# Moving the gating-weight loads of a fused attention and gated-MLP kernel to ScalarE's DMA queue, with a new timetable for the attention units

## The chip, the cores and the metric

The kernel runs on one core of one Trainium2 chip, in one launch. The metric is the device time of that launch in microseconds (us). Everything is computed in fp32; where a product needs it, an operand is split into a rounded part ("hi") and the rest ("lo"), and three matmuls (hi·hi, hi·lo, lo·hi) stand for one.

## The reference

Chunked attention in 8 heads over 4608 tokens (8 sequences of 576, chunks of 64, head size 64), then an RMS norm and a gated MLP (model width 512, inner width 1536):

```python
scores = scale * np.matmul(q_c, k_c.transpose(0, 1, 2, 4, 3))     # 64x64 per chunk
attn = softmax(scores)
out = np.matmul(attn, v_c)                                        # x: 4608 x 512
xn = x / sqrt(mean(x * x) + 1e-06) * rms_g
g = xn @ w_gate                                                   # 512 -> 1536
result = (silu(g) * (xn @ w_val)) @ w_out                         # 1536 -> 512
```

## The kernel before, in words

**Stages.** The 4608 tokens are nine tiles of 512. The first three ("plain" tiles) go through the MLP as ordinary matrix products. The other six go two by two, as three *pairs*, through a Strassen-Winograd scheme: seven block products P1 to P7 instead of eight. A pair has an *up* part (gate and value weights, `up_pair`, six groups `i` of seven products, 42 *steps*) and a *down* part (output weights, `down_pair`, again 42 steps). In the up part the products of a group come in the order `FIRST` for i = 0 and `ORD` (P1 P6 P5 P7 P2 P4 P3) otherwise, so step s is product s mod 7 of group s // 7. An up step is 12 matmuls of 128x128 by 128x512 (`product`, L751), a down step 6 of them (L925).

**Attention in between.** While a pair is computed, the attention of the next pair's tokens is done in four *units* of 256 tokens, unit 0 to 3. `unit_steps` gives the ten pieces of a unit: load q and k; scores on TensorE, then the two exponentials on ScalarE (`first`, L340); load v; sums and a VectorE transpose (`second`); write the weights to DRAM (`away`, L362, two transfers); read them back turned (`third`, L371, eight transfers); attention values on TensorE (L388) and the norm, which uses VectorE (L402), ScalarE (L455, L410) and GpSimd (`fourth`); a VectorE transpose (L416); write x to DRAM (L421); read it back (L428, four transfers). Unit n starts at up step `PAIR_AT[n]`, and piece k comes at the end of up step `PAIR_AT[n] + PAIR_STEPS[k]`; what falls on step 42 or later goes to down step 2·(step - 42), ahead of that step's product. The last pair has no units.

**Order of work.** In the pairs the order on SyncE's queue (SP), VectorE and ScalarE is the order in which the program is written; TensorE's too. All transfers of the pairs are issued from SP, one after the other: an issue that waits holds back all issues behind it. In the compiled program the transfers, whatever queue issues them, take eight completion counters in turn, and an issue waits until the transfer eight places earlier in the program has landed.

**Weights.** The block weights of the up part lie in DRAM as 21 *rings* (`wsd`, 1 MB, two products each) and are loaded into a pool of 18 buffers (`wts`, 8 KB a partition) that also holds the inputs of the products (`xp`), the gated results (`g`) and the output weights (`wo`). A buffer is taken in the order in which buffers were given back. At the start of each product, `ring_load_ahead(n // 2)` brings the loads up to three rings ahead; from group 1 on this puts one ring load at the start of each even step s, and the ring is first used at step s + 4. The first three rings of the next pair are loaded at down step 34. The output weights are loaded by `out_load` in 14 *slots* per pair of four or two blocks. P5, P6, P7 and P3 come from `wol` in one transfer a slot; P1, P2 and P4 (`AS_IS`) are cut out of `wod` with one transfer of 256 KB per block. `out_load` runs three slots ahead; slots 0 and 1 are loaded at up steps 39 and 41.

**Down part.** Each down step uses a gated block split into hi (ScalarE, `gh`, L848) and lo (VectorE, `gl`, L849). `split_next` runs four ahead: the first four splits are at up steps 35, 37, 39 and 41 (`G_AT`). `less` (L885) adds a VectorE subtraction to down steps 2 to 7, 9 to 14 and 20 to 25. `start(5)` (L1200) is one more VectorE subtraction just before down step 0.

## Time and profile before

| | |
|---|---|
| runs (median, lowest, highest) | 924.67, 922.69, 924.72 us |
| the profiled execution's own time | 925.69 us |
| its span, first to last instruction | 923.9 us |
| granted TensorE clock, mean | 0.996 |
| TensorE matmul busy | 887.3 us (96%) |
| VectorE / ScalarE / GpSimd busy | 644.0 / 444.6 / 127.4 us |
| transfers | 233.41 MB, mean 253 GB/s |
| ring loads `wr<-wsd` | 63 of 1024 KB, median 8.2 us from issue to landing |
| output weights `wo<-wod` | 54 of 256 KB, median 6.9 us |

In the profile's rows, L751 is line 751 of the kernel; `ps_a<-xp,wr` is a matmul into the tile ps_a from xp and wr. PE is TensorE's matmuls, PEld its weight loads, DVE VectorE, ACT ScalarE, POOL GpSimd, SPq the queue of SyncE, ACTq that of ScalarE. A number in brackets with an arrow, `[1.39 <-DMA wr<-wsd]`, is idle time of the engine just before the row, and what ended it. The table of windows has, for each stretch of time, the busy time of each engine with its instructions in brackets, then the granted clock, the busy share of the DMA engines and their rate.

### The profile page before, as it was taken

To read this page: it belongs to the slowest core of one execution; us is meant where nothing else is said; L and a number is where in the kernel's file an instruction comes from. 1 tells how busy PE (TensorE), PEld (TensorE's weight loads), DVE (VectorE), ACT (ScalarE), POOL (GpSimd) and SP (SyncE) were. 2 spreads that over 40 slices of the span, in tenths; PEclk is the share of its full clock that TensorE was granted. 3 is DMA by queue.
4 is the path that set the end of the run, shared out by engine and by line. 5 is a ranking of instruction groups with operands and counts; after the bars stand their busy time and mean duration, and the time that the engine had idled before them with its cause. 6 is when DMAs were issued, how large, how long until landed. Compare 5 with 4: busy or idle time off the path is not lost.

```text
span 923.9 us, 17389 instructions
## 1 busy us (share of the span) xinstructions
PE 887.3 (96%) x6828; PEld 724.4 (78%) x6828; DVE 644.0 (70%) x1071; ACT 444.6 (48%) x731; POOL 127.4 (14%) x141
## 2 busy tenths in 40 slices
PE   5799999999999999999998999999999999999998
PEld 4578878887887878878876788887787888888886
DVE  6999986465587554856775987676589974444885
ACT  5988944353456564433453643344355532212452
POOL 0100012233300000121221000221220002211000
PEclk9999999999999999999999999999999999999999
DMA  9698989877997762668795868478688777345713
GB/s 352 275 330 304 365 314 344 290 248 220 292 328 230 224 187 78 250 228 293 246 326 201 298 260 315 177 251 310 258 283 276 257 286 315 142 141 165 264 47 136
DMA packets 98226, 233.41 MB, mean 253 GB/s; under 512 B 9440, under 2 KB 61152, under 8 KB 85472
## 3 DMA queue, kind: packets, MB, share of 16 engines
q1 hardware_dynamic: 97088, 231.77, 71.4%
q8 instruction: 54, 0.88, 0.4%
q10 hardware_dynamic: 1056, 0.52, 0.2%
q14 instruction: 28, 0.23, 0.1%
HBM read 167.25 MB, written 65.01 MB: 251 GB/s over the span
## 4 chain that ended last, share of the span: by engine, by line
PE 65%; DMA 8%; DVE 5%; ACT 3%; SPq 2%; issue 2%; POOL 2%; ACTq 0%; DVEq 0%; POOLq 0%
PE ps_c L751 9%; PE ps_a L751 9%; PE ps_b L751 9%; PE ps_b L925 5%; PE ps_g L545 5%; PE acc L580 5%; PE ps_v L545 5%; PE ps_d L751 5%; PE ps_c L925 4%; PE ps_a L925 4%; PE ps_d L925 3%; DMA kt<-kT_dram 2%; DMA wo<-wol 2%; PE ps_o L388 1%; DMA away_e<-e 1%
## 5 line engine op out<-in xcount | busy, mean ns | idle before, releaser
L848 ACT CAST gh<-g 128x512 fp32r<-128x512 f32 x126 | 73.6, 619 | 71.4 <-PE ps_b L925 18.9
L751 PE MATMUL ps_a<-xp,wr 128*128 128x512 f32 x432 | 104.1, 390 | 2.3 <-DMA wr<-wsd 2.0
L751 PE MATMUL ps_c<-xp,wr 128*128 128x512 f32 x432 | 106.2, 395 | 0.0
L751 PE MATMUL ps_b<-xp,wr 128*128 128x512 f32 x432 | 103.8, 390 | 0.0
L849 DVE TENSOR_TENSOR gl<-g,gh 128x512 fp32r<-128x512 f32 x126 | 86.0, 687 | 23.2 <-ACT gh L848 21.8
L545 PE MATMUL ps_g<-xh,parts 128*128 128x512 f32 x288 | 98.2, 400 | 3.1 <-ACT sg L563 2.9
L545 PE MATMUL ps_v<-xh,parts 128*128 128x512 f32 x288 | 95.9, 393 | 0.5 <-DVE sg L567 0.5
L751 PEld LDWEIGHTS ps_a<-xp,wr 128*128 128x128 f32 x432 | 80.7, 188 | 19.8 <-issue 3.0
L751 PEld LDWEIGHTS ps_c<-xp,wr 128*128 128x128 f32 x432 | 81.7, 190 | 17.4
L751 PEld LDWEIGHTS ps_b<-xp,wr 128*128 128x128 f32 x432 | 80.8, 188 | 16.9
L580 PE MATMUL acc<-parts,gh 128*128 128x512 f32 x288 | 90.2, 394 | 0.0
L545 PEld LDWEIGHTS ps_g<-xh,parts 128*128 128x128 f32 x288 | 55.1, 191 | 16.3 <-ACT sg L563 4.0
L815 POOL TENSOR_TENSOR g<-c,c 128x512 f32<-128x512 f32 x18 | 23.2, 1290 | 308.8 <-DVE c L811 293.1
L545 PEld LDWEIGHTS ps_v<-xh,parts 128*128 128x128 f32 x288 | 54.7, 190 | 12.5 <-DVE sg L567 1.0
L580 PEld LDWEIGHTS acc<-parts,gh 128*128 128x128 f32 x288 | 53.1, 188 | 11.4 <-ACT gh L568 0.2
L791 ACT ACTIVATE c<-c 128x512 f32<-128x512 f32 x18 | 11.4, 633 | 96.9 <-DVE c L811 96.9
L545 PE MATMUL ps_g<-xl,parts 128*128 128x512 f32 x144 | 57.2, 397 | 0.0
L545 PE MATMUL ps_v<-xl,parts 128*128 128x512 f32 x144 | 56.5, 392 | 0.0
L580 PE MATMUL acc<-parts,gl 128*128 128x512 f32 x144 | 56.3, 391 | 0.0
L751 PE MATMUL ps_d<-xp,wr 128*128 128x512 f32 x216 | 52.2, 390 | 0.0
L567 DVE TENSOR_TENSOR sg<-ps_v,sg 128x512 f32<-128x512 f32 x36 | 24.6, 683 | 32.4 <-PE ps_v L545 28.6
L751 PEld LDWEIGHTS ps_d<-xp,wr 128*128 128x128 f32 x216 | 40.3, 188 | 8.6
(143 smaller groups left out, 1677.4 us busy)
## 6 DMA issues: line engine op xcount, KB each, us to landing
wr<-wsd SPq DMA_DIRECT2D x63, 1024.0 KB, 8.2
wo<-wod SPq DMA_DIRECT2D x54, 256.0 KB, 6.9
raw<-w_up_dram SPq DMA_DIRECT2D x12, 1024.0 KB, 7.8
wo<-wol SPq DMA_DIRECT2D x12, 1024.0 KB, 7.5
vt<-v_dram SPq DMA_DIRECT2D x18, 512.0 KB, 5.8
wsd<-parts SPq DMA_DIRECT2D x18, 512.0 KB, 7.5
qt<-qT_dram SPq DMA_DIRECT2D x17, 512.0 KB, 6.0
kt<-kT_dram SPq DMA_DIRECT2D x17, 512.0 KB, 6.9
```

The source lines that it names most:

```text
L388: nc.tensor.matmul(st["o"][(2 * c + t) * Q : (2 * c + t + 1) * Q, h * D : (h + 1) * D], eT[c][rows, t, h], vt[rows, c, h], start=True, sto ...
L545: nc.tensor.matmul(ps, a[f][:, cols], b[dt], start=(dt == 0 and i == 0), stop=(dt == NDT - 1 and i == 2),)
L567: nc.vector.tensor_tensor(sg, pv, sg, op=ALU.mult)
L580: nc.tensor.matmul(acc[s], a[:, cols], b, start=(f == 0 and i == 0), stop=(f == NF - 1 and i == 2),)
L751: nc.tensor.matmul(ps, w[:, a, m, cols], xp[:, b, kt], start=start and kt == 0 and i == 0, stop=stop and kt == 1 and i == 2, skip_group_ch ...
L791: nc.scalar.activation(t, t if src is None else src, AF.Silu)
L815: nc.gpsimd.tensor_tensor(g[:, 1, 1], kp["c22"], kept[0]["c22"], op=mult)
L848: nc.scalar.copy(gh, src)
L849: nc.vector.tensor_tensor(gl, src, gh.bitcast(F32), op=ALU.subtract)
L925: nc.tensor.matmul(ps[m][INTO[p]], w[:, m, a], parts[c], start=p in FROM and i == 0 and j == 0, stop=p in LAST and i == NPR - 1 and j == 2 ...
```

## The change

The ring loads inside the up part are issued from ScalarE's queue, at the same place in the program (the start of the product). The next pair's first three rings are loaded one by one at down steps 24, 28 and 32, still from SP, instead of all at step 34. `wod` becomes one DRAM tensor, so that a slot of P1, P2 or P4 is one transfer of 1 MB or 512 KB instead of four or two of 256 KB. The units start at steps 3, 13, 23, 33 instead of 5, 14, 23, 32, and the last four pieces of a unit come one step later. With that, unit 3's `fourth` and the VectorE transpose after it move from up steps 40 and 41 to down steps 0 and 2, and its write and read of x from down steps 0 and 2 to 4 and 6. The scaling of the first half of x (`x1`) moves from up steps 35 and 36 to 30 and 31.

```diff
-PAIR_STEPS = -4, 0, 1, 2, 3, 4, 8, 9, 10, 11
-PAIR_AT = 5, 14, 23, 32
+PAIR_STEPS = -4, 0, 1, 2, 3, 4, 9, 10, 11, 12
+PAIR_AT = 3, 13, 23, 33
...
-EARLY_AT = (35, "x1"), (36, "x1")
+EARLY_AT = (30, "x1"), (31, "x1")
...
+RING_AT = 24, 28, 32
...
-    wod = [dram.tile([P, 4 * DM], F32, name=f"wod{n}") for n in range(NPR)]
+    wod = dram.tile([P, NPR, 4 * DM], F32, name="wod")
...
-        nc.sync.dma_start(wod[i], flat(out_parts[i]).bitcast(F32))
+        nc.sync.dma_start(wod[:, i], flat(out_parts[i]).bitcast(F32))
...
-    def ring_load(n):
+    def ring_load(n, queue):
         if n < len(wsd):
             t = ring[n] = big([P, 2, 2, 2, KH], F32R, "wr")
-            nc.sync.dma_start(t.rearrange("p n a m c -> p n (a m c)").bitcast(F32), wsd[n])
+            queue.dma_start(t.rearrange("p n a m c -> p n (a m c)").bitcast(F32), wsd[n])
...
-            ring_load_ahead(n // 2)
+            ring_load_ahead(n // 2, nc.scalar)
...
-    def ring_load_ahead(n):
+    def ring_load_ahead(n, queue=nc.sync):
         while loaded[0] < min(n + AHEAD_R, len(wsd)):
-            ring_load(loaded[0])
+            ring_load(loaded[0], queue)
             loaded[0] += 1
...
         if ns[0][0] in AS_IS:
-            for j, (p, i) in enumerate(ns):
-                part = wod[i].rearrange("p (a n c) -> p a n c", a=2, c=KH)[:, :, AS_IS[p]]
-                nc.sync.dma_start(t[:, j].rearrange("p (a c) -> p a c", a=2).bitcast(F32), part)
+            p, i = ns[0]
+            part = wod[:, i : i + len(ns)].rearrange("p j (a n c) -> p j a n c", a=2, c=KH)
+            to = t[:, : len(ns)].rearrange("p j (a c) -> p j a c", a=2)
+            nc.sync.dma_start(to.bitcast(F32), part[:, :, :, AS_IS[p]])
...
-            down_at.setdefault(7 * NPR - 8, []).append(lambda: ring_load_ahead(0))
+            for n, k in enumerate(RING_AT):
+                down_at.setdefault(k, []).append(lambda n=n: ring_load_ahead(n + 1 - AHEAD_R))
```

## The prediction

> **What bounds the kernel now.** I read the page first (TensorE busy 96% of the span, clock 0.996), then a table of windows with one row for the up part and one for the down part of each pair, because nothing before the first pair changes but six stores.

> ```profile
> core 0: us, PE busy (x) PEld busy (x) DVE busy (x) ACT busy (x) POOL busy (x), PEclk, DMA share, GB/s
> 369.57:503.59 134.02, 128.37 (x1274) 104.46 (x1272) 90.38 (x157) 54.79 (x89) 27.07 (x32) 0.99 0.74 264
> 503.59:561.54 57.95, 57.41 (x253) 47.23 (x252) 50.00 (x75) 31.39 (x52) 0.00 (x0) 1.00 0.73 263
> 561.54:690.14 128.60, 126.94 (x1273) 103.94 (x1272) 89.97 (x157) 52.41 (x84) 26.49 (x32) 1.00 0.75 266
> 690.14:748.62 58.48, 57.57 (x253) 47.15 (x252) 50.00 (x75) 32.57 (x54) 0.55 (x1) 1.00 0.72 252
> 748.62:863.02 114.40, 114.40 (x506) 94.78 (x505) 57.53 (x82) 26.35 (x43) 20.63 (x16) 1.00 0.62 223
> ```

> TensorE is the bound in every row, at full clock. Its idle time is the only thing that a change of order can win: 5.65 us in the first up part, 0.54, 1.66 and 0.91 in the next three, none in the last pair, which has no units. Together 8.8 us. The waits of TensorE from 369 us on say what these are:

> ```profile
> PE ps_o L388 <- issue: 3.1, 1, 3.1
> PE ps_a L751 <- DMA wr<-wsd: 2.0, 2, 1.4
> PE ps_b L925 <- DMA wo<-wol: 1.5, 2, 0.9
> PE ps_s L263 <- DMA kt<-kT_dram: 1.1, 2, 0.8
> PE ps_s L263 <- issue: 0.8, 1, 0.8
> PE ps_a L751 <- issue: 0.3, 1, 0.3
> ```

> So 4.6 us are late transfers (2.0 + 1.5 + 1.1), once in each pair each. The other 4.2 us are "issue", gaps inside the short attention matmuls in which no wait shows.

> Why the transfers are late stands in the timelines of SP's queue and of TensorE around unit 2 of the first pair:

> ```profile
> 450.98 0.43 SPq L743 DMA_DIRECT2D wr<-wsd  x1
> 452.92 1.92 SPq L362 DMA_DIRECT2D away_e<-e  x2
> 458.76 3.61 SPq L371 DMA_DIRECT2D eT<-away_e  x8
> 462.42 0.42 SPq L743 DMA_DIRECT2D wr<-wsd  x1
> 463.36 0.43 SPq L233 DMA_DIRECT2D kt<-kT_dram  x1
> ```

> ```profile
> 464.63 1.48 PE L388 MATMUL ps_o<-vt,eT 64*32 64x64 f32 x128
> 467.50 2.96 PE L751 MATMUL ps_a<-xp,wr 128*128 128x512 f32 x12 [1.39 <-DMA wr<-wsd]
> 471.31 1.16 PE L263 MATMUL ps_s<-kt,qt 64*64 64x64 f32 x64 [0.85 <-DMA kt<-kT_dram]
> 520.65 0.47 PE L925 MATMUL ps_b<-gh,wo 128*128 128x512 f32 x1 [0.54 <-DMA wo<-wol]
> ```

> SP has written the attention weights out at 452.92 and cannot read them back until they have landed, at 458.76. The ring load and the q and k loads of unit 3 stand behind that: they leave at 462.4 to 463.4, and TensorE waits for both. In the chain of waits the write takes 5.83 us, kt 7.82 us and the late output load 8.22 us (the last row is six down steps, 1.36 us each):

> ```profile
> 452.92 5.83 DMA away_e<-e
> 463.36 7.82 DMA kt<-kT_dram
> 512.30 8.22 DMA wo<-wol
> 529.07 8.16 PE ps_a L925 x36
> ```

> Asked for single issues, the profile gives 2.0 us to landing for such a write on an idle queue (393.3 us) and 5.0 us for the ring load of 462.42, against a median of 8.2 for all ring loads on the page:

> ```profile
> DMA to landing us min/median/max: 2.0/2.0/2.0
> DMA to landing us min/median/max: 5.0/5.0/5.0
> wr<-wsd SPq DMA_DIRECT2D x63, 1024.0 KB, 8.2
> ```

> So 3.8 us of the write's 5.83 are the 1 MB ring load issued 2 us ahead of it and the rest of what went before.

> **The change part by part.**

> *Ring loads on ScalarE's queue.* At unit 2 the write no longer stands behind the ring of 450.98 in one queue. It lands between 2.0 and 5.83 us after 452.92; I take 3, since the two still share the engines. Then the reads go out from about 456, q and k leave near 460 instead of 463, and kt has until the scores, which come one step later: the 0.85 us goes, and likewise in the second pair. The ring load of step 28 must wait on its counter for the first of the eight reads (eight places earlier), about 456 + 2 = 458. It lands at 463, before step 32 (464.5): the 1.39 us goes. Taken: -2.0 and -1.1.

> What it costs: 18 issues of 0.42 us in each pair's steps on ScalarE, 7.6 us, where ScalarE is idle 79 us of 134 (first row). But ScalarE works in order, and here the load can now be late or hold up others (rows of TensorE's and ScalarE's timelines):

> ```profile
> 442.61 3.02 PE L751 MATMUL ps_b<-xp,wr 128*128 128x512 f32 x12
> 447.45 0.63 ACT L340 ACTIVATE e<-e 128x512 f32<-128x512 f32 x1 [0.95 <-DVE e L334]
> 453.66 2.88 PE L751 MATMUL ps_a<-xp,wr 128*128 128x512 f32 x12
> 456.78 1.05 ACT L797 COPY p<-ps_a 128x512 f32<-128x512 f32 x2
> 663.65 3.02 PE L751 MATMUL ps_d<-xp,wr 128*128 128x512 f32 x12
> 669.45 0.63 ACT L340 ACTIVATE e<-e 128x512 f32<-128x512 f32 x1 [0.94 <-DVE e L334]
> ```

> (a) At steps 14, 24 and 34 the ring load stands right behind the two exponentials of units 1, 2 and 3. At unit 2 the second exponential starts at 447.45, 4.8 us after step 24 started (442.61), and the ring is needed at step 28 (453.66). That leaves 6.2 us from its start, 5.6 from its end, for a landing of 5.0. At unit 3 of the second pair (669.45, its step started at 663.65) it is 5.2 and 4.6. Best case 0; with each of the six late by the difference to the median of 8.2, 2.6 us each, 15.6. The nearest rows are the 5.0 us loads, since ScalarE's queue holds nothing but rings: I take 0.4 for each unit 3 and 0 for the rest, +0.8.

> (b) At step 28 the two copies of 456.78 stand behind the ring load's wait, to about 458.5. They feed a VectorE sum that must be done before step 31 (461.8): 458.5 + 0.55 + 0.7 leaves 2 us. Taken 0. With the write at its old 5.83 us the wait lasts to about 461, and the bound is +0.5 a pair. Units 0 and 1 have the same wait at steps 8 and 18, with nothing behind it that is due so soon.

> (c) In the last pair ScalarE is idle 88 of 114 us and there is no other traffic: each ring has four products, 11 us (442.61 to 453.66), for a 5.0 us landing. Nothing.

> *Later pieces of unit 3.* `fourth` moves to down step 0. Rows of the second pair, where no gap disturbs it:

> ```profile
> 687.33 1.29 DVE L402 TENSOR_TENSOR xu<-ps_o,rs 128x512 f32<-128x512 f32 x2
> 690.34 0.69 DVE L823 TENSOR_TENSOR u<-ps_c,u 128x512 f32<-128x512 f32 x1 [0.67 <-PE ps_c L751]
> 690.73 0.72 ACT L410 ACTIVATE xu<-xu,ri_t 128x512 f32<-128x512 f32 x1 [0.23 <-POOL ri_t L458]
> 692.62 1.24 DVE L416 STREAM_TRANSPOSE xu<-xu 128x1024 f32<-128x1024 f32 x1
> 694.35 0.68 DVE L1200 TENSOR_TENSOR g<-g 128x512 f32<-128x512 f32 x1
> 694.95 1.52 DVE L849 TENSOR_TENSOR gl<-g,gh 128x512 fp32r<-128x512 f32 x2
> ```

> From the start of xu to the end of the second scaling 4.1 us pass (687.33 to 691.45). In the new order VectorE has u, g, gl and L1200 first, 0.6 us apart (694.35 to 694.95), so xu starts at 690.34 + 2.4 = 692.7 and ScalarE is free at 696.9. Only then comes the cast for down step 4 and its lo part: 698.1. TensorE reaches that step at 690.14 + 1.5 (ps_o, row 464.63) + 4 x 1.36 = 697.1 and wants the lo part at its second matmul, so it waits about 0.8. With the transpose (1.24) ahead of the lo part of step 6, another 0.4. That is 1.2 us in the second pair. In the first pair the 3.1 us issue gap falls into the same attention matmuls and VectorE catches up meanwhile: 0. Taken +1.2, bounds 0 and 2.4.

> *Output weights.* The 0.54 us at 520.65, and 0.91 in the second pair, are P6's first load (8.22 us in the chain), queued behind x's read-back and two 256 KB pieces. Now that load goes out before the read-back and behind one 512 KB piece issued long before: -1.5. In exchange slot 0 stands behind unit 3's eight reads, which take SP 3.61 us (row 458.76) and now come one step, 2.7 us, nearer to its use: taken 0, bound +1 a pair. The bytes are the same. Six stores into one tensor instead of six: nothing, nobody waits for them for 300 us.

> *Next rings at 24, 28, 32, x1 at 30, 31.* Three 1 MB loads leave up to 14 us earlier, spread between output loads, into a stage with DMA share 0.73; buffers have long been given back by then. Four scalings fall on idle ScalarE time. Nothing, either way.

> *Issue gaps* (4.2): the instruction stream of TensorE keeps its length, so I keep them; they could go, or come elsewhere.

> **Sum.** -2.0 - 1.1 - 1.5 + 0.8 + 1.2 = -2.6 us on the profiled 925.69, which makes 923.1. That execution lies 1.0 us above the median of 924.67 (span 923.9 plus 1.8 around it), so the forecast for the median is 922.1.

> [...] The row first: the load of 462.42 landed in 5.0 us, so it was late by its place in SP's order, not by the engines. [...]

> **Rivals.**
> *Nothing repaid:* all late transfers go, (a) and the down part cost nothing, and the 3.1 gap closes, for it fell among the first output loads: 924.7 - 4.6 - 3.1 = 917.0; without the gap 920.1. For it: ScalarE and VectorE are idle half the time or a third. Against: the down rows above.
> *No effect:* the transfers are late by bandwidth. the waits of 2.0 and 1.1 stay, the output load's 1.5 goes, the down part costs 1.2: 924.7 - 0.3 = 924.4. Against: 5.0 us alone.
> *Rings late behind the exponentials (slower):* kt landed at 471.2, 3.8 us after the ring load ahead of it (467.4), for 1 MB of q and k. If x's read-back of 512 KB, which leaves just then, shares with the ring, half of that, 1.9, is added: 6.9 to landing against some 5.6 of lead. 1.3 x 6 = 7.8 instead of 0.8, thus 922.1 + 7.0 = 929.1. It decides as soon as such a ring takes more than about 6 us.

> **How the numbers follow.** Forecast 0.45 (918.5 for a full gain less repayment to 925, by the bounds of the terms), nothing repaid 0.2, no effect 0.15, late rings 0.2. About 0.3% (2.8 us) is what can be told from no change: below 921.9 or above 927.4. The forecast lies at that border: 0.2 of its 0.45 is faster, 0.25 same. Faster 0.2 + 0.2 = 0.40; same 0.25 + 0.12 + 0.03 = 0.40; slower 0.17 + 0.03 = 0.20. Range 918.0 to 929.0, cutting the ends of the first and the last rival.

> **What would show it.** Right: no TensorE wait for wr, kt or wol at the three places; away_e of unit 2 landing in about 3 us; ring loads as ACTq rows at 1 per two steps; a wait for gl or gh of about 1 us near down step 4 of the second pair. Wrong: idle time "<-DMA wr<-wsd" at steps 18, 28 or 38; ScalarE waiting for eT reads; ps_o at down step 0 waiting for its reads, or slot 0 arriving late; new issue gaps.

## The result, and the profile after

The changed kernel takes 936.32 us (median; 934.29 to 937.62), the kernel before beside it 924.69 (922.69 to 924.76): a ratio of 1.0129, 95% interval 1.0106 to 1.0152. It is slower by 11.6 us, where 2.6 us less were forecast. The profiled execution took 936.09 us, span 934.3.

The table of windows for the changed kernel, the up and down parts of the first two pairs (columns as before):

```profile
core 0: us, PE busy (x) PEld busy (x) DVE busy (x) ACT busy (x) POOL busy (x), PEclk, DMA share, GB/s
371.64:504.33 132.69, 128.22 (x1273) 104.96 (x1271) 90.48 (x157) 52.70 (x83) 25.48 (x28) 0.99 0.75 254
504.33:562.84 58.51, 58.06 (x259) 47.26 (x253) 49.64 (x76) 33.13 (x56) 1.58 (x4) 1.00 0.80 279
562.84:700.16 137.32, 129.38 (x1274) 104.87 (x1272) 92.83 (x161) 52.53 (x83) 25.46 (x28) 0.99 0.72 244
700.16:759.00 58.84, 58.84 (x252) 48.52 (x253) 47.50 (x71) 32.67 (x56) 1.58 (x4) 0.97 0.74 262
```

The four stretches add up to 387.4 us against 379.1 before: 8.3 of the 10.4 us that the span grew. Most of it is the second pair's up part (137.3 against 128.6). The other 2.1 us lie ahead of the pairs, where the two programs differ in six stores only. In the profiles of all kernels of this study with full ring loads the first pair starts between 368.1 and 372.7 us, so these 2.1 us cannot be told from chance. The last pair is as it was. TensorE's waits in the pairs:

```profile
PE ps_s L264 <- DMA kt<-kT_dram: 3.5, 1, 3.5
PE ps_c L752 <- issue: 3.3, 1, 3.3
PE ps_c L927 <- DVE xu L403: 2.3, 1, 2.3
PE ps_s L264 <- issue: 2.2, 2, 1.3
PE ps_o L389 <- DMA eT<-away_e: 1.0, 1, 1.0
PE ps_c L927 <- ACT gh L849: 0.2, 1, 0.2
PE ps_c L927 <- DVE gl L850: 0.2, 1, 0.2
```

No ring load is late any more and no P6 output load. But the sum is 12.7 us, against 8.8 before, and other transfers are late. Around unit 2 of the first pair, SP's queue, then ScalarE's, then TensorE:

```profile
455.60 1.91 SPq L363 DMA_DIRECT2D away_e<-e  x2
461.81 4.93 SPq L372 DMA_DIRECT2D eT<-away_e  x8
466.84 0.37 SPq L233 DMA_DIRECT2D qt<-qT_dram  x1
467.26 0.43 SPq L234 DMA_DIRECT2D kt<-kT_dram  x1
```

```profile
459.69 0.33 ACTq L744 DMA_DIRECT2D wr<-wsd  x1
460.34 1.07 ACT L798 COPY p<-ps_a 128x512 f32<-128x512 f32 x2 [0.80 <-DMA x<-away_x]
466.66 0.33 ACTq L744 DMA_DIRECT2D wr<-wsd  x1
467.11 1.34 ACT L714 ACTIVATE x<-x,g_col 128x512 f32<-128x512 f32 x2 [5.69 <-DMA eT<-away_e]
467.80 0.33 ACTq L744 DMA_DIRECT2D wr<-wsd  x1
```

```profile
478.13 2.05 PE L264 MATMUL ps_s<-kt,qt 64*64 64x64 f32 x64 [3.51 <-DMA kt<-kT_dram]
```

The write takes 6.2 us (455.60 to 461.81, when the reads can go), though no ring load stands ahead of it in SP's queue. Two had left the other queue at 450.13 and 451.46, and the second takes 8.9 us, so the write runs beside it. The next goes out at 459.69, and the reads run beside that one. q and k leave at 467 instead of 463 (counted from the start of the first pair, 1.8 us later than before), together with two ring loads (466.66, 467.80). 3 MB start within 1.2 us, and k lands 10.7 us later, against 7.8 before:

```profile
DMA to landing us min/median/max: 10.7/10.7/10.7
```

The view of DMA issues over the first pair's up part says the same of all of them (median us to landing last). Before, then after:

```profile
away_e<-e SPq DMA_DIRECT2D x8, 256.0 KB, 4.7
eT<-away_e SPq DMA_DIRECT2D x32, 64.0 KB, 2.0
```

```profile
away_e<-e SPq DMA_DIRECT2D x8, 256.0 KB, 5.6
eT<-away_e SPq DMA_DIRECT2D x32, 64.0 KB, 4.6
```

The worst read is in the chain of waits of the second pair, 10.67 us in a place where TensorE then waits:

```profile
590.16 10.67 DMA eT<-away_e
```

The waits explain 3.9 of the 8.3 us. The rest is mostly TensorE's clock. Of the rows below, the first two are two neighbouring windows of the changed kernel at the late kt; the next two lie around a late kt of 2.8 us in the kernel with only the queue changed (`queue_only`, below):

```profile
475.11:478.52 3.41, 0.39 (x16) 0.41 (x19) 1.48 (x2) 2.49 (x3) 1.26 (x1) 1.00 0.42 168
478.52:481.93 3.41, 3.41 (x58) 2.95 (x57) 1.82 (x5) 0.19 (x1) 0.00 (x0) 0.50 0.89 279
```

```profile
468.12:471.53 3.41, 1.67 (x8) 1.05 (x6) 0.04 (x1) 2.72 (x7) 1.85 (x5) 1.00 0.78 305
471.53:474.94 3.41, 2.37 (x70) 2.11 (x71) 2.99 (x5) 1.30 (x2) 0.00 (x0) 1.00 0.95 351
```

In the first pair TensorE was busy for 0.39 of 3.41 us, and for the next 3.41 us it got half its clock (0.50), which costs 1.7 us. In the second the same kind of wait fell across two windows, and the clock stayed at 1.00. The four stretches hold one such half-clock window before and three after: 3.4 us. That makes 7.3 of the 8.3; the last 1.0 us I can't place.

### The profile page after: what moved, and what is told of

It is laid out like the page before. It is cut to its first block, busy times and chain, and to the rows that moved or that the text cites. A ratio compares the mean times of both kernels' runs of the same rounds, so it can differ in the third digit from the quotient of the medians.

```text
span 934.3 us, 17302 instructions
## 1 busy us (share of the span) xinstructions
PE 889.1 (95%) x6828; PEld 725.4 (78%) x6828; DVE 644.0 (69%) x1071; ACT 444.8 (48%) x731; POOL 128.4 (14%) x141
## 4 chain that ended last, share of the span: by engine, by line
PE 71%; DMA 9%; DVE 8%; ACT 5%; issue 3%; POOL 2%; SPq 2%; ACTq 0%; DVEq 0%; POOLq 0%
PE ps_c L752 9%; PE ps_b L752 9%; PE ps_a L752 9%; PE ps_g L546 6%; PE acc L581 6%; PE ps_v L546 6%; PE ps_a L927 5%; PE ps_b L927 5%; PE ps_c L927 5%; PE ps_d L752 4%; DMA eT<-away_e 3%; PE ps_d L927 3%; PE ps_s L264 2%; DMA kt<-kT_dram 2%; PE ps_o L389 1%
## 5 line engine op out<-in xcount | busy, mean ns | idle before, releaser
L849 ACT CAST gh<-g 128x512 fp32r<-128x512 f32 x126 | 73.3, 619 | 67.5 <-DVE gl L850 17.7
L801 DVE TENSOR_TENSOR u<-ps_b,p 128x512 f32<-128x512 f32 x36 | 24.6, 689 | 37.0 <-PE ps_b L752 28.2
L927 PE MATMUL ps_c<-gh,wo 128*128 128x512 f32 x144 | 47.0, 400 | 2.5 <-DVE xu L403 2.3
L792 ACT ACTIVATE c<-c 128x512 f32<-128x512 f32 x18 | 11.4, 632 | 77.9 <-DVE c L812 77.9
## 6 DMA issues: line engine op xcount, KB each, us to landing
wr<-wsd ACTq DMA_DIRECT2D x54, 1024.0 KB, 6.2
raw<-w_up_dram SPq DMA_DIRECT2D x12, 1024.0 KB, 7.7
wo<-wol SPq DMA_DIRECT2D x12, 1024.0 KB, 7.7
wr<-wsd SPq DMA_DIRECT2D x9, 1024.0 KB, 8.5
wo<-wod SPq DMA_DIRECT2D x9, 1024.0 KB, 9.9
```

The costliest lines, as they stand in the source:

```text
L792: nc.scalar.activation(t, t if src is None else src, AF.Silu)
L801: nc.vector.tensor_tensor(kp["u2"], b["b"], kp["p1"], op=add)
L849: nc.scalar.copy(gh, src)
L927: nc.tensor.matmul(ps[m][INTO[p]], w[:, m, a], parts[c], start=p in FROM and i == 0 and j == 0, stop=p in LAST and i == NPR - 1 and j == 2 ...
```

## The experiments

**Theories.** 1: with the ring loads on a second queue they run beside the small transfers of the attention weights (away_e, eT) and beside q and k, and make those late. 2: the new timetable costs the time. A third part, the single wod tensor, was tried alone.

### One part at a time

`queue_only`: before, with the ring loads on ScalarE's queue.

```diff
...
-            ring_load_ahead(n // 2)
+            ring_load_ahead(n // 2, nc.scalar)
...
```

> The kernel before with nothing changed but the queue of the up part's ring loads (ScalarE's). Theory 1 (sharing): eT reads at a median of 4 us or more, away_e above 5, late kt or late eT waits and with them 929 to 936. Theory 2 (timetable): the late waits for wr and kt of before (2.0 and 1.1 us) go and nothing comes, 921 to 925.

935.72 us, ratio 1.0111 (1.0072 to 1.0150): by itself it costs what the whole change costs, as far as the intervals tell. The profile (an execution of 930.92 us) has no half-clock window in the pairs. TensorE's waits in the pairs, and the reads:

```profile
PE ps_s L263 <- DMA kt<-kT_dram: 7.7, 4, 2.8
...
PE ps_o L388 <- DMA eT<-away_e: 2.2, 3, 1.4
```

```profile
eT<-away_e SPq DMA_DIRECT2D x32, 64.0 KB, 4.0
```

The 2.0 us for wr are gone as forecast, and 7.7 for kt and 2.2 for eT stand in their place. Theory 1 holds (only the write, 4.8 us, is not quite "above 5"), theory 2's 921 to 925 does not.

`all_but_queue`: the changed kernel with that line turned back.

```diff
-            ring_load_ahead(n // 2, nc.scalar)
+            ring_load_ahead(n // 2, nc.sync)
```

> The changed kernel with the up part's ring loads back on SP's queue; the new timetable, the single wod tensor and the early next rings stay. Theory 1 (the ring loads on the second queue run beside the small attention transfers and delay them): eT reads in the first pair's up part land in about 2 us at the median as before (after: 4.6), no wait of 3.5 us for kt at unit 3 of the first pair, time 922 to 927. Theory 2 (the timetable, ten apart and the last piece in the down part, costs it): the time stays at 932 to 937 and the gaps of 3.3 and 2.3 us in the second pair stay.

928.85 us, 1.0047 (1.0018 to 1.0076): between the two theories, and 2 us above theory 1's 922 to 927. The reads are back at 1.9 us and the late kt is gone, so the queue made those. By the interval two to seven us stay. Late ring loads are most of the waits now, 6.3 us against 2.0 before:

```profile
PE ps_a L752 <- DMA wr<-wsd: 3.3, 2, 2.8
PE ps_b L752 <- DMA wr<-wsd: 3.0, 2, 1.7
```

`units_only`: before, with the two lines of the timetable.

```diff
-PAIR_STEPS = -4, 0, 1, 2, 3, 4, 8, 9, 10, 11
-PAIR_AT = 5, 14, 23, 32
+PAIR_STEPS = -4, 0, 1, 2, 3, 4, 9, 10, 11, 12
+PAIR_AT = 3, 13, 23, 33
```

> The kernel before with only the units' new timetable (start 3, 13, 23, 33; last pieces one step later). Theory 1 (sharing): within 3 us of before, 922 to 927, eT reads near 2 us. Theory 2 (timetable): 932 to 937, with a wait of ps_c or gl of 2 us at the start of the second pair's down part.

928.06 us, 1.0041 (1.0012 to 1.0070); eT at 1.9. I expected no difference above 3 us, and it is 3.6 by the medians. With odd starts every unit's reads are issued just ahead of a ring load, where before those of two units in four were. Two ring loads in each pair are now late instead of one (2.2 + 0.8 us for wr in all).

`after_old_units` (the changed kernel with the old two lines) and `after_fourth_up` (the changed kernel with the old PAIR_STEPS alone; in the diff its only line is the first pair):

```diff
-PAIR_STEPS = -4, 0, 1, 2, 3, 4, 9, 10, 11, 12
+PAIR_STEPS = -4, 0, 1, 2, 3, 4, 8, 9, 10, 11
-PAIR_AT = 3, 13, 23, 33
+PAIR_AT = 5, 14, 23, 32
```

> The changed kernel with the old timetable of the units (start 5, 14, 23, 32, old steps of the last pieces); queue, wod and early next rings stay. Theory 1 (sharing): the loss stays, 930 to 937, with eT at 3.5 us or more. Rival (the timetable is what costs in the changed kernel): 922 to 927.

> The changed kernel with the last four pieces of a unit one step earlier again (+8 to +11), so that unit 3's values and norm stay in the up part; the starts stay at 3, 13, 23, 33. If the gap of 2.3 us at the first down step of the second pair comes from that piece's place, it goes, 931 to 934. Rival (the reads are late there and TensorE waits for them one step earlier instead): 934 to 938, with waits of ps_o for eT.

937.54 us, 1.0146 (1.0105 to 1.0188), just above theory 1's range, and 934.22, 1.0133 (1.0094 to 1.0173). With the rings on the second queue the timetable neither costs nor saves what can be told: 1.0129 lies in both intervals. In after_fourth_up it came as its rival says: TensorE waits for eT, one step earlier, for 10.2 us in all. There, too, the gap at the first down step of the second pair stayed (2.5 us, now named a wait for wo<-wol), so it isn't the place of the norm.

`wod_only`: before, with the single wod tensor and one transfer a slot, by the lines of the change.

```diff
-    wod = [dram.tile([P, 4 * DM], F32, name=f"wod{n}") for n in range(NPR)]
+    wod = dram.tile([P, NPR, 4 * DM], F32, name="wod")
...
-                nc.sync.dma_start(t[:, j].rearrange("p (a c) -> p a c", a=2).bitcast(F32), part)
+            nc.sync.dma_start(to.bitcast(F32), part[:, :, :, AS_IS[p]])
```

> The kernel before with only the single wod tensor and one transfer a slot. If the two waits for the first P6 output load (0.54 and 0.91 us) are queueing behind the small pieces, they go: 923.2, faster by 1.5 us or 0.16%. Rival (a transfer of 512 KB or 1 MB lands later than its quarters, and the down parts grew by 0.4 to 0.6 us each in the changed kernel): 925 to 926.

923.88 us, 0.9994 (0.9972 to 1.0016), no difference by its interval. The two waits for wo<-wol did go from the trace; issue gaps at ps_s of 2.9 us, against 0.8 before, stand in it instead.

`after_again`: the changed kernel as it is.

> The changed kernel once more, unchanged. Theory 1 (sharing between the two queues): again 934 to 938, with kt and eT waits in the pairs; the 4 us that it lost in the first 12 us of its profile (a kT load of 11.4 us) do not come again, since nothing of the program differs there. Rival (the start is slower for a reason in the changed program): the wait of about 5 us for kT at the start comes again.

933.29 us, 1.0105 (1.0066 to 1.0145), just under the 934 expected. The waits came again at the same places (kt 3.9, issue 3.3, down step 0 2.3), but not the 1.0 for eT. The wait for kT at the start came again too, smaller (2.8 us after 5.0), against what I expected; after_kt_early, whose start is the same, had none. So it comes and goes with the execution, and I don't count it as a cost of the change.

### Is it the bytes?

`queue_half_rings` and `sp_half_rings`: each ring load brings the high parts only, from ScalarE's queue or from SP's. The low parts of the gate and value weights are left out.

```diff
...
-            queue.dma_start(t.rearrange("p n a m c -> p n (a m c)").bitcast(F32), wsd[n])
+            half = wsd[n].rearrange("p n (a c) -> p n a c", a=2)
+            queue.dma_start(t.rearrange("p n a m c -> p n a (m c)")[:, :, 0].bitcast(F32), half[:, :, 0])
...
-                    w[:, a, m, cols],
+                    w[:, 0, m, cols],
```

> The kernel before with the up part's ring loads on ScalarE's queue, and every ring load cut to half its bytes: the low parts of the gate and value weights are left out, and the products use the high part in their place, with the same matmuls. Theory 1 (the bytes of the ring loads stand in the way of the small transfers): the median eT read falls from 4.0 to 3 us or less, the kt waits of 7.7 us shrink below 2, time 918 to 925. Rival (it is the shared counters and the order of the two queues, not the bytes): eT reads stay near 4, time 930 or more.

> The control of the half ring loads: the kernel before, ring loads all on SP, each cut to half its bytes (the low parts of the gate and value weights are left out, the high part is used in their place). Theory 1 (the second queue costs time only by the bytes that it puts beside the small transfers): with half the bytes the queue costs nearly nothing, so this one lies within 3 us of the 917.6 of the same cut on ScalarE's queue, 915 to 920. Rival (the queue costs about 11 us whatever the bytes): 905 to 909. And if the gaps without a wait in the attention matmuls come from a busy memory system, they are gone here too, 0 instead of 4.2 us.

917.60 us, 0.9929 (0.9911 to 0.9947), and 916.44, 0.9934 (0.9909 to 0.9958). With half the bytes the second queue costs nothing that can be told, where it cost 11 us. So it isn't the queue as such, nor ScalarE's order, nor the shared counters, but what the queue puts beside the small transfers when there are many bytes. The reads still differ, 3.5 us (ScalarE's queue) and 2.0 (SP's), so my "3 or less" was too low; at these bytes little of that reaches TensorE. For each of the two, the reads' landing in the first pair's up part and a row of TensorE's waits:

```profile
eT<-away_e SPq DMA_DIRECT2D x32, 64.0 KB, 3.5
```

```profile
PE ps_o L388 <- DMA eT<-away_e: 1.3, 2, 1.2
```

```profile
eT<-away_e SPq DMA_DIRECT2D x32, 64.0 KB, 2.0
```

```profile
PE ps_s L263 <- issue: 2.0, 2, 1.8
```

The first has no issue gap, the second 2.0 us, so my "0" for the second was wrong too. The last section says what the traces show of these gaps.

### Which of the two is on the second queue?

`small_on_act`: before, with the pairs' away_e and eT on ScalarE's queue, rings on SP.

```diff
-        nc.sync.dma_start(away, st["e"].rearrange("p t h k -> p (t h k)"))
+        weights_queue[0].dma_start(away, st["e"].rearrange("p t h k -> p (t h k)"))
...
-                nc.sync.dma_start(eT[c][dst].rearrange("p t h q -> p t (h q)"), back[c, k])
+                weights_queue[0].dma_start(eT[c][dst].rearrange("p t h q -> p t (h q)"), back[c, k])
...
+    weights_queue[0] = nc.scalar
```

> The kernel before with the ring loads left on SP and the pairs' attention weights (away_e and its reads, 10 small transfers a unit) on ScalarE's queue instead. Theory 1 (what counts is that the small transfers and the ring loads run from two queues at once, whichever is on which): eT reads at a median of 3.5 us or more, away_e at 4 or more, 928 to 936. Rival (what counts is that ScalarE issues the ring loads late or in bursts): eT reads near 2 us, the waits for wr go since SP is never held up by the reads, 920 to 925.

958.47 us, 1.0377 (1.0333 to 1.0421), far beyond both expectations. The reads took 4.3 us, as theory 1 says. Much of the size comes from something else that I had left out: ScalarE now stands at the reads until the write has landed (its writes took 5.5 us at the median in the first up part; one wait in the first pair is 10.7 us), and its copies and what VectorE makes of them are late. So this run doesn't decide between the two.

```profile
eT<-away_e ACTq DMA_DIRECT2D x28, 64.0 KB, 4.3
```

```profile
PE ps_o L390 <- DMA eT<-away_e: 14.2, 5, 6.9
PE ps_b L753 <- DVE u L802: 11.9, 4, 4.2
```

### Does more lead hide it?

`after_kt_early`: the changed kernel with q and k two steps earlier.

```diff
-PAIR_STEPS = -4, 0, 1, 2, 3, 4, 9, 10, 11, 12
+PAIR_STEPS = -6, 0, 1, 2, 3, 4, 9, 10, 11, 12
```

> The changed kernel with the q and k loads of units 1 to 3 two up steps (5.4 us) earlier. Theory 1: the reads still share the engines (eT at 3.5 to 4.6), but the late kt of 3.5 us goes and with it a half-clock stretch of 3.4 us: 928 to 933. Rival (the price is eT and what follows it, not kt): 934 to 937.

935.10 us, 1.0129 (1.0081 to 1.0177): no gain, in the rival's range and above theory 1's 928 to 933. But the edit didn't give the lead that I meant it to give. At step -6 q and k stand right behind the previous unit's reads, and SP gets there only when the write has landed:

```profile
460.66 4.69 SPq L372 DMA_DIRECT2D eT<-away_e  x8
465.87 0.43 SPq L234 DMA_DIRECT2D kt<-kT_dram  x1
```

```profile
DMA to landing us min/median/max: 10.3/10.3/10.3
```

```profile
476.34 2.02 PE L264 MATMUL ps_s<-kt,qt 64*64 64x64 f32 x64 [2.46 <-DVE xu L417]
```

Counted from the start of the first pair, k left 0.6 us earlier than in the changed kernel, not 5.4. It landed at 476.2, just before the matmuls at 476.34, so this gap is the late kt again, whatever the row names. Other kt waits are 3.3 us. The run says nothing about what a real lead would do.

`queue_kt_ahead4`: before, with single wod, q and k two steps earlier, ring loads four ahead, the rings on ScalarE's queue.

```diff
-AHEAD_R = 3
+AHEAD_R = 4
...
-PAIR_STEPS = -4, 0, 1, 2, 3, 4, 8, 9, 10, 11
+PAIR_STEPS = -6, 0, 1, 2, 3, 4, 8, 9, 10, 11
...
-            ring_load_ahead(n // 2)
+            ring_load_ahead(n // 2, nc.scalar)
```

> The version with early q and k, single wod and four rings ahead, but with the up part's ring loads on ScalarE's queue. Theory 1 in its strong form (the reads that land late cost by themselves): eT at 3.5 us or more, waits of ps_o for eT of 2 us or more, 926 to 932. Rival (only kt was short of lead; with the lead of two steps the queue costs nothing): 919 to 923.

946.07 us, 1.0263 (1.0227 to 1.0300), worse than either expectation. Here q and k do leave ahead of the reads, and no kt is late. But with earlier rings, q and k, more megabytes are under way when the reads go:

```profile
eT<-away_e SPq DMA_DIRECT2D x24, 64.0 KB, 6.5
```

```profile
PE ps_o L388 <- DMA eT<-away_e: 11.8, 7, 3.4
PE ps_o L388 <- DMA wr<-wsd: 7.3, 2, 3.7
```

So the late transfer that was taken away uncovered the next. The same kernel with its rings on SP is `wod_kt_ahead4` below, 0.9980: the queue alone makes this difference.

### The order on one queue

All of these keep the rings on SP. `reads_after_ring`: single wod, and the reads one step later, so that they leave right behind a ring load. q and k are one step earlier and stand ahead of the reads as well.

```diff
-PAIR_STEPS = -4, 0, 1, 2, 3, 4, 8, 9, 10, 11
+PAIR_STEPS = -5, 0, 1, 2, 3, 5, 8, 9, 10, 11
```

> The kernel before with rings on SP, the single wod tensor, and two pieces of the pairs' units moved by one step: the reads of the attention weights leave behind the next ring load instead of ahead of it (step +5, not +4), and q and k one step earlier (-5). If the waits for wr and kt of before (2.0 and 1.1 us) come from the ring load that stands in SP's order behind reads that wait for their write, they go: 920 to 922. Rival (each late transfer hands its lateness on to the next one): 924 to 928.

928.66 us, 1.0046 (1.0017 to 1.0075), not 920 to 922; the rival's 924 to 928 was nearer. The waits for wr and kt went, as expected, and the reads paid for it, 6.0 us on one queue, behind a ring load and q and k:

```profile
eT<-away_e SPq DMA_DIRECT2D x32, 64.0 KB, 6.0
```

```profile
PE ps_o L388 <- DMA eT<-away_e: 4.4, 6, 1.7
```

`wod_kt_early` (single wod and the last pair of lines below) and `wod_kt_ahead4` (all four lines):

```diff
-AHEAD_R = 3
+AHEAD_R = 4
...
-PAIR_STEPS = -4, 0, 1, 2, 3, 4, 8, 9, 10, 11
+PAIR_STEPS = -6, 0, 1, 2, 3, 4, 8, 9, 10, 11
```

> The kernel before with rings on SP, the single wod tensor, and q and k of units 1 to 3 two up steps earlier; the reads of the weights stay where they were. The waits for kt (1.1 us) and wol (1.5) go, the two for wr (2.0) stay: 921.5 to 923.5. Rival (the earlier q and k loads stand ahead of a ring or a write and make those late): 925 to 928.

> As the one with early q and k, and ring loads four ahead instead of three, so that a ring load has two more steps (5.4 us) before its first product. The waits for wr (2.0) go as well, 919 to 921.5. Rival (the fourth ring load ahead only fills the pool of 18 buffers and waits for one to come free): the same as with three ahead.

922.55 us, 1.0007 (0.9985 to 1.0029), and 921.12, 0.9980 (0.9957 to 1.0004); neither differs from before by its interval. Both times lie in the ranges expected, but only because the kernel before took 922.30 beside them. In the first the waits for kt and wol went and those for wr grew from 2.0 to 4.0 us; in the second these went too. q and k now stand ahead of the reads, which took 4.4 and 4.5 us.

`ahead4`: single wod and four rings ahead, nothing else.

```diff
-AHEAD_R = 3
+AHEAD_R = 4
```

> The kernel before with the single wod tensor and ring loads four ahead instead of three; q and k where they were. The waits for wr (2.0 us) and wol (1.5) go, those for kt (1.1) stay: 920.5 to 922.5, that is 2 to 4 us less than the kernel before on the same chip. Rival (a ring load that is no longer late hands its wait to kt, which stands behind it): the kt waits grow by as much, no difference to before.

921.05 us, 0.9977 (0.9957 to 0.9997), as expected, if barely clear of no change. No wait for wr; one late kt of 1.8 us left, and the reads at 2.1.

`ahead4_kt5`: the same with q and k at -5. That puts them right behind the previous unit's reads and ahead of the next ring load.

```diff
-AHEAD_R = 3
+AHEAD_R = 4
...
-PAIR_STEPS = -4, 0, 1, 2, 3, 4, 8, 9, 10, 11
+PAIR_STEPS = -5, 0, 1, 2, 3, 4, 8, 9, 10, 11
```

> Rings on SP four ahead, the single wod tensor, and q and k one up step earlier, which is right behind the previous unit's reads of the attention weights and ahead of the next ring load. Theory 1 (what is issued ahead in the same queue decides): eT reads stay at 2.0 to 2.5 us, no wait for kt, wr, wol or eT, 919.5 to 921.5, 2 to 4 us under the kernel before. Rival (any megabyte near the reads slows them, ahead or behind): eT at 4 us or more, 921 to 924.

919.73 us, 0.9951 (0.9935 to 0.9967): faster than the kernel before, and than the changed one. Whether the order adds to the longer lead isn't shown, since this interval and that of `ahead4` overlap. Of TensorE's waits in the pairs one row is left, and no transfer in it:

```profile
eT<-away_e SPq DMA_DIRECT2D x32, 64.0 KB, 1.9
```

```profile
PE ps_s L263 <- issue: 4.7, 3, 2.0
```

## Why the prediction was wrong, step by step

**Ring loads on the second queue (-2.0, -1.1).** The first half was right: the waits for wr went. The step that failed is the next one: "I take 3, since the two still share the engines" for the write, after which "q and k leave near 460 instead of 463". Unit 2's write took 6.2 us and q and k left at 467, 1.8 us later than before when counted from the first pair's start. The reads weren't priced at all: I let them land in the 2.0 us of before, and it was 4.6. The -1.1 for kt became a wait of 3.5, which is +2.4. That price was in the trace of before. Its reads at unit 1 run behind a ring load in the same queue, those of unit 2 alone, here from the answers on the eT reads at 427 to 430 and 459 to 462 us:

```profile
DMA to landing us min/median/max: 3.4/4.4/5.0
```

```profile
DMA to landing us min/median/max: 1.8/1.9/2.0
```

I had read the wait of SP's queue for the write as pure loss. It also kept the ring load out of the way of the reads, and q and k ahead of the next ring. The second queue took that order away.

**No effect, the rival.** That nothing was to be gained from a second queue is borne out (1.0111 by itself), and lateness by bandwidth fits: with half the bytes the loss went (917.60 us with the second queue, 916.44 without). The rival was still 12 us too low (924.4 against 936.32), since it kept the old order. Nor did the small write get past the ring loads from its own queue: 5.6 us at the median in the first up part, against 4.7.

**(a) Rings behind the exponentials (+0.8), and the slower rival.** 0: no ring load was late at steps 14, 24 or 34. My rival on the slower side had the right sign by a mechanism that didn't occur. **(b)** 0 for the copies, as taken, but not by the working given: the counters are taken in the order of the compiled program (in the trace of before, each of the 574 issues that take a counter again takes that of the transfer eight places earlier, and none starts before that one has landed), and there the ring load of step 28 doesn't stand behind all eight reads, as it does in the source. It waited for a transfer of x's read-back, which landed at 459.67 (issued at 450.82, 8.8 us), and left at 459.69, ahead of the reads. That it was in time, near the 458 of the forecast, was luck. The next one, of step 30, was held until a read had landed (462.18 to 466.63; it left at 466.66, with ScalarE idle for 5.7 us by the row at 467.11), so it went out together with q and k.

**Later pieces of unit 3 (+1.2).** The waits for gh and gl are 0.2 + 0.2. **Output weights (-1.5, bound +1 for slot 0).** The P6 waits went, but slot 0 came late by more than the bound:

```profile
694.98 0.85 SPq L864 DMA_DIRECT2D wo<-wol  x2
```

```profile
700.16 0.56 PE L927 MATMUL ps_c<-gh,wo 128*128 128x512 f32 x1 [2.27 <-DVE xu L403]
```

The row names VectorE's norm, which isn't an operand of this matmul; after_again names wo<-wol at the same gap, and here slot 0 landed 5.0 us after its issue, at 700.0. It left at 694.98, behind reads that had waited for a write of 8.6 us beside two ring loads:

```profile
DMA to landing us min/median/max: 6.9/7.7/8.6
```

So most of this 2.3 is again the price of the second queue. The timetable has a part in it: in all_but_queue, with the rings on SP, the second pair has no such wait, but the first pair one of 0.9 us for wo<-wol, about the bound of +1.

**Issue gaps (4.2, kept).** 5.5, at other places. **The clock** was in no term: +3.4 us in the pairs. The 2.1 us ahead of the pairs are within what that stretch varies by. With kt +2.4 instead of -1.1, slot 0 +2.3, eT +1.0, gh and gl +0.4 instead of +2.0 for (a) and the later pieces, issue +1.3 and the clock +3.4, the sum would have read slower by about 7 us, above the range.

## What to carry to other kernels

Here a queue that waited also kept large loads out of the way of small, dependent transfers (reads of 2.0 us at the median, 4.0 with the ring loads on a second queue). Before moving the large ones to a second queue, look in the trace for the same small transfer alone and beside a large one (here 1.9 and 4.4 us) and ask whether its consumer has that much slack. Here the late loads were better mended on one queue, by a longer lead for the bulk loads together with this order: small dependent reads first, then what is needed next, then the bulk (`ahead4_kt5`, 0.9951). And when an edit gives a transfer more lead, look in the trace whether it really leaves earlier: in after_kt_early k left 0.6 us earlier, not 5.4.

## What the runs showed of the hardware that I had not expected

The issue gaps have a counterpart in the traces. The profile's list of DMA queues has one, q8, of the kind "instruction": 54 packets of 16 KB over the whole program. In the profiles of before and after the pairs hold six issue gaps of TensorE of more than 0.3 us (0.33, 3.08 and 0.81 us; 0.91, 3.34 and 1.27 us). Each of the six ends 1.2 to 1.5 us after a packet of that queue has ended, and each lies in or within 3 us behind the attention's short matmuls (64 in 1.1 us, against 12 in 2.7 us for a product). The two stretches hold 24 such packets each, so most come with no gap, and no run moved one: what TensorE waits for there is not shown.
